# Two GpSimd drains among the last output scatters of a block-causal attention and mixture-of-experts kernel

## The chip, the cores and the metric

The kernel runs on one core of one Trainium2 chip, as one program with one launch. The metric is the device time of an execution in microseconds (us). Before the change the median of three executions is 787.66 us (785.13 to 788.49).

## The reference, cut to what matters

Attention of 8 batches and 8 heads with 576 positions of 64 elements comes first. Its mask is by blocks of 64 positions: a position sees its own block and all earlier ones. The 4608 rows of 512 elements that result are then sent to experts, each row to one expert, and each of the 8 experts takes 576 rows.

```python
attn = softmax(scale * q @ k.T, block-causal)          # 8 x 8 x 576 x 576
x = (attn @ v).transpose(0, 2, 1, 3).reshape(4608, 512)
logits = x @ w_gate                                    # 4608 x 8
for idx in np.argsort(-logits.flatten()):              # best pair (row, expert) first
    tok, e = idx // 8, idx % 8
    if assigned[tok] < 0 and counts[e] < 576: assigned[tok] = e; counts[e] += 1
for e in range(8):
    mask = assigned == e
    out[mask] = np.maximum(x[mask] @ w1[e], 0) @ w2[e] # 512 -> 1024 -> 512
```

## The kernel before, in words

The program has two stages. In the first, heads are worked off in pairs: TensorE makes the scores, VectorE and ScalarE the softmax, GpSimd a part of the scaling, and the result goes to a DRAM tensor `x` in 16-bit halves (a high part and a rest). In the second, a routing step finds for expert number `k` (0 to 7, in the order in which the routing fills them) the list of its 576 rows, the tile `ix`. Then the expert itself runs, and the next expert's routing runs beside it.

For each expert GpSimd (POOL) has three kinds of work. `gather` (L1006) fetches the expert's rows from `x` by five indirect DMAs, four of 128 rows and one of 64. `weights` (L977) makes the low halves of the weights, eight subtractions of 128x1024. `yev`, inside `ffn`, puts the results out: for each of five row tiles `m` TensorE finishes `y` (L1082, and L1086 for the tile of 64 rows), ScalarE scales it into the tile `yo` (L1065), for `m==4` VectorE adds a second half to it (L1069), and GpSimd issues one indirect DMA that scatters the rows of `yo` to the output in DRAM (L1073). That makes 40 gathers and 40 scatters in the program. The last expert takes its row tiles in the order 0, 1, 2, 4, 3, the others in the order 0 to 4; the fifth scatter of expert 6 is thus its tile of 64 rows, and so is the fourth scatter of expert 7.

All instructions are placed when the program is built. A greedy planner (class `Sched`) holds a model of the engines; every step is a generator that yields an engine, a cost and the events that it needs, and the planner decides which step comes next on which engine. What an engine then does at run time is its own list in that order, with semaphore waits between engines. What a step issues between two yields is placed together, and an instruction without a yield of its own has no cost in the planner's model.

Behind the last instruction the program has a closing part, put there by the context manager and shown in the profile under the line of the `_run` call (L1146): each engine drains, SyncE waits for the DMAs that are still out, all engines meet at a barrier, GpSimd clears the semaphores, and they meet again. The same kind of opening stands at the start under L1137.

Of the kernel before, what the change touches and what calls it, by code (L numbers as in the profile page):

```python
# [614 lines left out]
class Moe:  # L615
# [419 lines left out]
    def ffn(s,k):  # L1035
        nc=s.nc; fp=s.fp; sc=s.sc
        yield S,0,('xm',k,0),('xm',k,1 if k else 0),*[('wc',k,n) for n in range(4) if k or n==0]
        (W,Y),X=s.W[k],s.X[k]
        HH=fp.tile([P,8,576],F16,tag="HH",name=f"HH{k}",bufs=1); HL=fp.tile([P,8,576],F16,tag="HL",name=f"HL{k}",bufs=1)
        def hev(f,h,ps,gk,ts):  # L1040
            w=ts.stop-ts.start
            yield A,51+.835*w
            nc.scalar.activation(HH[:,f,ts],ps,AF.Relu)  # L1043
            yield D,69+1.042*w
            nc.vector.scalar_tensor_tensor(HL[:,f,ts],ps,0.0,HH[:,f,ts],op0=OP.max,op1=OP.subtract)  # L1045
            sc.set(('h',k,8*h+f)); sc.set(gk)
        for h,ts in enumerate((slice(0,256),slice(256,576)) if k else (slice(0,128),slice(128,576))):
            w=ts.stop-ts.start
            for f0 in range(0,8,4):
                pg={}  # L1050
                nf=4 if k==0 and h==0 and f0==0 else 1
                for f,d in [(f,d) for a in range(f0,f0+4,nf) for d in range(4) for f in range(a,a+nf)]:
                    yield T,3*(w/2.4+3),'g' if d==0 else None,('g2',k-1),*[('xm',k,m) for m in range(1,5) if h],('wc',k,d) if k==0 else None
                    if d==0: gk=sc.gtake(); pg[f]=s.ps.tile([P,512],F32,tag="g",name=f"h{k}_{f}_{h}",bufs=4)[:,:w],gk
                    ps,gk=pg[f]
                    for n,(a,l) in enumerate(((0,0),(0,2),(1,0))):
                        nc.tensor.matmul(ps,lhsT=W[:,a,d,f*P:f*P+P],rhs=X[:,4*(d//2)+d%2+l,ts],start=(d==0 and n==0),stop=(d==3 and n==2))  # L1057
                    sc.nolat()
                    if d==3: sc.add(hev(f,h,ps,gk,ts),1,sc.now+200)
        sca=1.0/(s.XS*s.WS*s.WS)  # L1060
        def yev(m,ps,gk):
            n=P if m<4 else 64
            yield A,478
            y=fp.tile([P,512],F32,tag="y",name=f"yo{k}_{m}",bufs=3)
            nc.scalar.activation(y[:n],ps[P-n:],AF.Copy,scale=sca)  # L1065
            if m==4:

                yield D,603
                nc.vector.scalar_tensor_tensor(y[:n],ps[:n],sca,y[:n],op0=OP.mult,op1=OP.add)  # L1069
            sc.set(gk)  # L1070

            yield G,1038,('yo',s.ny-1),('gi',1) if k==0 and m>1 else None
            nc.gpsimd.indirect_dma_start(out=s.out,out_offset=bass.IndirectOffsetOnAxis(ap=s.ix[k][:n,m:m+1],axis=0),in_=y[:n],in_offset=None)  # L1073

            sc.soft(728,('yo',s.ny)); sc.ev['yo',s.ny]=max(sc.ev['yo',s.ny],sc.now+4500); s.ny+=1
        for m in range(5) if k+1<s.E else (0,1,2,4,3):
            if m==0: sc.set(('mid',k))
            for f in range(8 if m<4 else 4):
                yield T,645 if m<4 else 720,*[(x,k,y) for g in ((f,) if m<4 else (f,f+4)) for x,y in (('h',g),('h',8+g),('wc',4+g//2))],'g' if f==0 else None
                if f==0: gk=sc.gtake(); ps=s.ps.tile([P,512],F32,tag="g",name=f"y{k}_{m}",bufs=4)  # L1080
                for n,(Z,a) in enumerate(((HH,0),(HH,1),(HL,0))):
                    if m<4: nc.tensor.matmul(ps,lhsT=Z[:,f,m*P:m*P+P],rhs=Y[:,a,f],start=(f==n==0),stop=(f==7 and n==2))  # L1082
                    else:

                        for g in range(2):
                            nc.tensor.matmul(ps[64*g:64*g+64],lhsT=Z[:,4*g+f,512:576],rhs=Y[:,a,4*g+f],start=(f==n==0),stop=(f==3 and n==2))  # L1086
                sc.nolat()
            if m==4: sc.set(('g2',k)); sc.set(('ffn',k))
            sc.add(yev(m,ps,gk),1,sc.now+200)
        if k+1<s.E: sc.add(s.ffn(k+1),3,sc.now)  # L1090
# [59 lines left out]
```

## Time and profile before

| what | value |
|---|---|
| three executions | 787.66 us median, 785.13 to 788.49 |
| the profiled execution's own time | 789.05 us |
| its span in the trace | 787.3 us |
| granted TensorE clock, mean over the span | 0.968 |

The span is the time from the first to the last record of the trace; 1.75 us of the profiled execution's own time lie outside it. Start times count from the span's start. POOL, ACT, DVE, PE and SP are GpSimd, ScalarE, VectorE, TensorE and SyncE; a name with a q behind it (POOLq, SPq) is the engine's own sequencer, whose rows (drains, semaphore waits) are not counted as busy time. The row of an indirect DMA on POOL is the time that GpSimd takes to issue it; the transfer itself is seen in the view of the DMA queues.

### The profile page before, as it was taken

The page shows a single profiled execution, that of the slowest core. Times are in us where ns is not written, and L with a number is a line of the kernel's source. Part 1 is how long each engine was busy: PE and PEld are TensorE (multiplying, and loading weights), DVE is VectorE, ACT ScalarE, POOL GpSimd, SP SyncE. Part 2 cuts the span into 40 slices and gives each one's busy share as a digit, 9 for nine tenths or more (in the row PEclk, how much of TensorE's full clock was granted, in tenths as well). Part 3 has the DMA queues.
Part 4 walks back from the last instruction along what each step waited for, and adds up shares of the span by engine and source line. Part 5 has one row for each costly group of instructions (what it writes and reads, how often), then busy time and mean ns, then how long its engine had stood idle before and what let it go on. Part 6 is the DMA issues. An engine that isn't in the chain of part 4 may idle for free.

```text
span 787.3 us, 19016 instructions
## 1 busy us (share of the span) xinstructions
PE 719.1 (91%) x6528; PEld 479.5 (61%) x6528; DVE 564.6 (72%) x2310; ACT 539.7 (69%) x1455; POOL 466.8 (59%) x509
## 2 busy tenths in 40 slices
PE   5879998999999999936999999999999999999995
PEld 3656776667776677734545747647557475574752
DVE  6899888998899879566988978869577693420210
ACT  5688888888998898724836868594965848392210
POOL 5788877898889777413414447283751926675001
PEclk9799999999999999975999999999999999999998
DMA  9878999989998993246117076472935719772001
GB/s 202 162 151 167 217 190 223 165 158 223 202 204 177 221 185 77 78 120 206 69 52 278 8 245 150 176 194 67 272 84 191 171 62 263 259 161 61 21 22 39
DMA packets 244305, 121.51 MB, mean 154 GB/s; under 512 B 200816, under 2 KB 227312, under 8 KB 244208
## 3 DMA queue, kind: packets, MB, share of 16 engines
q1 hardware_dynamic: 238320, 101.42, 57.1%
q0 software_dynamic: 5888, 18.88, 7.6%
q8 instruction: 51, 0.84, 0.4%
q14 instruction: 46, 0.38, 0.2%
HBM read 71.32 MB, written 18.87 MB: 115 GB/s over the span
## 4 chain that ended last, share of the span: by engine, by line
PE 38%; issue 5%; DMA 4%; ACT 4%; POOL 2%; DVE 0%; POOLq 0%; SPq 0%; ACTq 0%; DVEq 0%
PE h L1057 20%; PE y L1082 15%; DMA raw<-in_moe_w_dram 2%; PE y L1086 2%; POOL xg L1006 2%; ACT ja L752 1%; DMA out_dram<-yo,ix 1%; ACT W L975 1%; DMA xg<-x,ix 1%; ACT raw L971 1%; POOL W L977 1%; PE pe L934 1%; PE tot L824 0%; ACT yo L1065 0%; ACT HH L1043 0%
## 5 line engine op out<-in xcount | busy, mean ns | idle before, releaser
L438 POOL TENSOR_TENSOR P<-P,m 128x320 f32<-128x320 f32 (+8 forms) x285 | 209.5, 769 | 49.8 <-DVE m L430 32.6
L1057 PE MATMUL h<-X,W 128*128 128x320 f16 (+3 forms) x1536 | 196.0, 287 | 0.0
L416 ACT ACTIVATE P<-psb,m 128x576 f32<-128x576 f32 (+8 forms) x288 | 149.4, 542 | 26.7 <-DVE m L409 17.4
L1057 PEld LDWEIGHTS <-W 128*128 128x128 f16 x1536 | 141.9, 98 | 42.0 <-issue 2.7
L1082 PE MATMUL y<-W,HH 128*128 128x512 f16 x512 | 152.3, 379 | 0.0
L405 DVE TENSOR_REDUCE m<-psb 128x1 f32<-128x576 f32 (+8 forms) x288 | 125.0, 481 | 12.9 <-PE psb L380 12.4
L977 POOL TENSOR_TENSOR W<-raw,W 128x1024 f16<-128x1024 f32 x56 | 118.2, 2135 | 24.4 <-ACT W L975 21.4
L463 PE MATMUL psb<-mident,P 128*128 128x128 f32 x800 | 107.6, 283 | 11.3 <-POOL P L438 4.2
L1073 POOL DMA_INDIRECT out_dram<-yo,ix x40 | 39.3, 982 | 114.1 <-ACT yo L1065 82.0
L380 PEld LDWEIGHTS <-qT 128*64 128x64 f16 x1408 | 77.9, 113 | 42.9 <-issue 28.4
L463 PEld LDWEIGHTS psb<-mident,P 128*128 128x128 f32 x800 | 88.6, 144 | 22.9 <-POOL P L438 7.0
L380 PE MATMUL psb<-kT,qT 128*64 128x288 f16 (+8 forms) x704 | 91.7, 286 | 10.9 <-ACT P L416 9.8
L498 PE MATMUL psb<-PT,V 128*64 128x448 f32 (+5 forms) x776 | 98.1, 391 | 1.9 <-DVE PT L446 1.5
L1006 POOL DMA_INDIRECT xg<-x,ix x40 | 41.8, 1044 | 96.4 <-DMA raw<-in_moe_w_dram 49.8
L1043 ACT ACTIVATE HH<-h 128x320 f16<-128x320 f32 (+3 forms) x128 | 52.1, 410 | 65.8 <-PE h L1057 57.7
L1082 PE MATMUL y<-W,HL 128*128 128x512 f16 x256 | 97.0, 379 | 0.0
L444 ACT ACTIVATE PT<-psb 128x512 f32<-128x512 f32 (+1 forms) x165 | 82.4, 592 | 5.6 <-PE psb L463 5.4
L1045 DVE SCALAR_TENSOR_TENSOR HL<-h,HH 128x320 f16<-128x320 f32 (+3 forms) x128 | 57.3, 452 | 40.1 <-ACT HH L1043 36.3
L380 PE MATMUL psb<-kS,qT 128*64 128x288 f16 (+8 forms) x704 | 83.8, 283 | 0.3 <-DVE kS L350 0.2
L1082 PEld LDWEIGHTS <-HH 128*128 128x128 f16 x512 | 46.9, 98 | 53.9 <-issue 2.8
L971 ACT ACTIVATE raw<-raw 128x512 f32<-128x512 f32 x112 | 67.0, 624 | 6.9 <-DMA raw<-in_moe_w_dram 6.9
L498 PEld LDWEIGHTS psb<-PT,V 128*64 128x64 f32 x776 | 49.6, 138 | 33.2 <-issue 24.4
(216 smaller groups left out, 1037.3 us busy)
## 6 DMA issues: line engine op xcount, KB each, us to landing
raw<-in_moe_w_dram SPq DMA_DIRECT2D x64, 512.0 KB
x<-XR SPq DMA_DIRECT2D x8, 1152.0 KB
kn<-in_k_dram SPq DMA_DIRECT2D x15, 576.0 KB
qn<-in_q_dram SPq DMA_DIRECT2D x15, 576.0 KB
V<-in_v_dram SPq DMA_DIRECT2D x64, 128.0 KB
V<-in_v_dram SPq DMA_DIRECT2D x16, 64.0 KB
xg<-x,ix POOLq DMA_INDIRECT x40
out_dram<-yo,ix POOLq DMA_INDIRECT x40
```

Source lines behind the costliest of these rows:

```text
L380: nc.tensor.matmul(out if len(K1.shape) == 2 else out.rearrange("p (r j) -> p r j", r=2), lhsT=A[:, h, 64 * i:64 * i + 64], rhs=K1, start= ...
L405: nc.vector.tensor_reduce(m[:, 0, c:c + 1], ps[:, o:o + 64 * (i + 1)] if g else s.part(ps, g, i, o), axis=AX.X if g else AX.XY, op=OP.max)
L416: nc.scalar.activation(out, in_, AF.Exp, bias=m[:, 1, c:c + 1], scale=s.ESC, accum_out=m[:, 2, c:c + 1])
L438: nc.gpsimd.tensor_tensor(sl, sl, m[:, 3, c:c + 1].to_broadcast([P, w]), op=OP.mult)
L444: s.nc.scalar.activation(out, in_, AF.Copy)
L463: nc.tensor.transpose(ps[:, a], s.Pb[n % s.NP][:, s.OFF[i] + 128 * j:s.OFF[i] + 128 * j + P], s.ident)
L498: nc.tensor.matmul(ps[64 * h:64 * h + 64, 64 * (i0 - b0):64 * (b1 - b0)], lhsT=vn[:, j, 2 * (n % 2) + h, :], rhs=pt[:, s.PTI[(j, i0)]:s.PT ...
L971: nc.scalar.activation(raw[:,x],raw[:,x],AF.Copy,scale=s.WS)
L977: nc.gpsimd.tensor_tensor(lw,raw,hi,op=OP.subtract)
L1006: nc.gpsimd.indirect_dma_start(out=xg[:n],out_offset=None,in_=s.xd,in_offset=bass.IndirectOffsetOnAxis(ap=ix[:n,m:m+1],axis=0))
L1057: nc.tensor.matmul(ps,lhsT=W[:,a,d,f*P:f*P+P],rhs=X[:,4*(d//2)+d%2+l,ts],start=(d==0 and n==0),stop=(d==3 and n==2))
L1082: if m<4: nc.tensor.matmul(ps,lhsT=Z[:,f,m*P:m*P+P],rhs=Y[:,a,f],start=(f==n==0),stop=(f==7 and n==2))
```

## The change

One line is added to `yev`. Behind the scatter of row tile 4, for the experts 6 and 7, GpSimd gets a drain instruction. It is issued without a yield, so that the planner does not know of it, and the order of all other instructions is the same as before on every engine. Lines below it have numbers that are higher by one (the closing part is at L1147).

```diff
@@ yev, behind the scatter (L1073)
             yield G,1038,('yo',s.ny-1),('gi',1) if k==0 and m>1 else None
             nc.gpsimd.indirect_dma_start(out=s.out,out_offset=bass.IndirectOffsetOnAxis(ap=s.ix[k][:n,m:m+1],axis=0),in_=y[:n],in_offset=None)
 
+            if m==4 and k>s.E-3: nc.gpsimd.drain()
             sc.soft(728,('yo',s.ny)); sc.ev['yo',s.ny]=max(sc.ev['yo',s.ny],sc.now+4500); s.ny+=1
```

The list of GpSimd from the end of expert 6 on is now: scatter of tile 4 of expert 6, drain, scatters of tiles 0, 1, 2 and 4 of expert 7, drain, scatter of tile 3 of expert 7, and then the drain of the closing part.

## The prediction

> **What bounds the kernel now.** I read the page's busy shares first, then the end of the chain of waits, then GpSimd's rows in order of time, then the rows of the closing part, because the change touches nothing but GpSimd's list in the last 60 us.
>
> From the page: TensorE carries the program.
>
> ```profile
> span 787.3 us, 19016 instructions
> PE 719.1 (91%) x6528; PEld 479.5 (61%) x6528; DVE 564.6 (72%) x2310; ACT 539.7 (69%) x1455; POOL 466.8 (59%) x509
> ```
>
> TensorE is busy for 91% of the span, so GpSimd, with 59%, matters only where TensorE has ended. That is the end. The last pieces of the chain of waits (start, length, what):
>
> ```profile
> 773.35 0.69 DVE yo L1069
> 774.33 2.60 DMA out_dram<-yo,ix
> 776.97 1.67 issue
> 778.64 1.20 POOLq L1146
> ```
>
> The chain runs through the last scatters into a piece of GpSimd's own sequencer in the closing part. It shows 1.20 us of that piece and stops at 779.84, while the span goes on to 787.3. What fills the rest is in the rows of line L1146, the closing part (count, then shortest/median/longest in ns, then first and last start in us):
>
> ```profile
> L1146 SPq EVENT_SEMAPHORE  x13: 17/28/28, 773.6 to 787.2; - x13
> L1146 POOLq EVENT_SEMAPHORE  x4: 17/17/17, 786.5 to 787.2; - x4
> L1146 POOLq DRAIN  x3: 45/108/7803, 778.6 to 787.0; - x3
> L1146 ACTq DRAIN  x2: 14/310/607, 778.0 to 786.7; - x2
> ```
>
> One of GpSimd's three closing drains takes 7.803 us. It is the first of them, since the chain starts its piece at 778.64, so it ends at 786.44. GpSimd's first barrier step follows at 786.5, and the span ends 0.8 us later. The drain is therefore the last thing that the barrier waits for. ScalarE's longest is 0.607 us and ends at 778.6 with its last copy. Now GpSimd's own rows in order of time (start, length, idle time before it in brackets):
>
> ```profile
> 729.00 0.96 POOL L1073 DMA_INDIRECT out_dram<-yo,ix  x1 [4.27 <-ACT yo L1065]
> 732.47 0.90 POOL L1073 DMA_INDIRECT out_dram<-yo,ix  x1 [2.51 <-DVE yo L1069]
> 760.52 0.96 POOL L1073 DMA_INDIRECT out_dram<-yo,ix  x1 [27.14 <-ACT yo L1065]
> 765.70 0.96 POOL L1073 DMA_INDIRECT out_dram<-yo,ix  x1 [4.22 <-ACT yo L1065]
> 770.83 0.96 POOL L1073 DMA_INDIRECT out_dram<-yo,ix  x1 [4.17 <-ACT yo L1065]
> 774.33 0.91 POOL L1073 DMA_INDIRECT out_dram<-yo,ix  x1 [2.54 <-DVE yo L1069]
> 778.88 0.96 POOL L1073 DMA_INDIRECT out_dram<-yo,ix  x1 [3.64 <-ACT yo L1065]
> ```
>
> The last scatter's row ends at 778.88 + 0.96 = 779.84. From there to the end of the drain at 786.44 are 6.60 us in which GpSimd has no row but the drain. Is it the transfer that the drain waits for? The DMA view of 779.9 to 782.3, in 40 slices of 0.06 us, and SyncE's rows in two windows (778.5 to 782.0, then 782 to 783) say no:
>
> ```profile
> DMA  0000000099598599799500000000000000000000
> DMA packets 80, 0.26 MB, mean 109 GB/s; under 512 B 16, under 2 KB 16, under 8 KB 80
> L1146 SPq EVENT_SEMAPHORE  x7: 28/28/28, 781.6 to 782.0; - x7
> L1146 SPq DRAIN  x2: 7/10/13, 782.2 to 782.2; - x2
> ```
>
> The last packet is through at 779.9 + 20 x 0.06 = 781.1. SyncE, which waits for the completion of each outstanding DMA in turn, gets the last one at 781.6 and stands at the barrier at 782.2. All that the output needs is done then; GpSimd's drain holds the program until 786.44, which is 4.2 us longer.
>
> **The change part by part.** The edit adds two drains to GpSimd's list and takes nothing away. What they do hangs on where the 6.60 us come from, and the trace of before has no drain among scatters. The nearest rows are the two ends of the bound. At the low end stands the opening drain under L1137, behind four memsets and ahead of any DMA:
>
> ```profile
> L1137 POOLq DRAIN  x1: 169/169/169, 0.3 to 0.3; - x1
> L1006 POOL DMA_INDIRECT xg<-x,ix x40 | 41.8, 1044 | 96.4 <-DMA raw<-in_moe_w_dram 49.8 <-DVE ix L944 19.1 <-ACT W L964 15.9
> L1073 POOL DMA_INDIRECT out_dram<-yo,ix x40 | 39.3, 982 | 114.1 <-ACT yo L1065 82.0 <-ACT HH L1043 6.9 <-DVE jk L810 6.8
> ```
>
> A drain with no indirect DMA ahead of it takes 0.169 us, and the two that follow the long one in the closing part, with no DMA between, take 0.108 and 0.045 us. The long one stands behind 40 gathers and 40 scatters with no drain in 787 us. So there are two readings, with a price f for the part of the 6.60 us that a drain pays each time behind a scatter. In the first, f is near nothing and the 6.60 us are a debt that grows with the indirect DMAs since the last drain: 6.60 / 80 = 0.083 us for each. In the second, f is the whole 6.60 us, whatever lies ahead. I take the first: rows of 0.9 to 1.0 us for issues that move only 128 rows leave it natural that some bookkeeping for each stays behind, and a fixed wait that goes on 4.8 us after the transfer's completion (781.6 to 786.44) has nothing in the trace to wait for. That is a choice between readings, not a measurement.
>
> Under the first reading:
> - The first added drain follows the scatter at 732.47, whose row ends at 733.37. It pays for 75 DMAs, 75 x 0.083 = 6.2 us, and ends at 739.6. Queued behind it on GpSimd is only the scatter at 760.52, which waits for ScalarE anyway. The cover is the gap of 27.14 us, in which TensorE works without GpSimd. Cost 0; without that cover it would be 6.2 us.
> - The second follows the scatter at 774.33, whose row ends at 775.24. It pays for 4 DMAs, 0.33 us, and ends at 775.6. Behind it waits only the last scatter, which starts at 778.88 when ScalarE's `yo` is there. The cover is 778.88 - 775.24 = 3.64 us. Cost 0.
> - The closing drain pays for one DMA: it ends at 779.84 + 0.08 = 779.9 in place of 786.44.
>
> What is late next is SyncE, at the barrier at 782.2. It does not move, since the last scatter doesn't. The view of the stretches (window, its length, then busy time of PE, PEld, DVE, ACT, POOL) shows the first cover and the empty end: in the gap behind expert 6 TensorE is busy throughout and GpSimd idle, and behind the last scatter no engine has work left:
>
> ```profile
> 733.40:760.50 27.10, 27.10 (x199) 19.23 (x198) 6.91 (x15) 6.78 (x16) 0.00 (x0) 1.00 0.03 6
> 779.84:787.30 7.46, 0.00 (x0) 0.00 (x0) 0.00 (x0) 0.00 (x0) 0.00 (x0) 0.61 0.09 35
> ```
>
> Behind the drain the closing part still takes 787.3 - 786.44 = 0.82 us (two barriers and the clearing of semaphores between them), and I add 0.05 us for the way of SyncE's signal. New end of the span: 782.23 + 0.05 + 0.82 = 783.1. The gain is 787.3 - 783.1 = 4.2 us, not 6.60, because SyncE's wait for the last scatter takes over. In the profiled execution that makes 789.05 - 4.2 = 784.85. The median of the runs is 1.39 us under that execution; the tail is the same instructions there, so I take the 4.2 us off the median: **783.5 us**.
>
> For a general f the sum has three pieces. Up to f = 2.4 (782.2 less 779.84) the closing drain still hides behind SyncE and the gain is the full 4.2. From 2.4 to 3.64 the gain is 6.60 - f. Above 3.64 the second added drain pushes the last scatter by f - 3.64 and the closing drain costs f again, so the time changes by (f - 3.64) + (f - 6.60) = 2f - 10.24: nothing is gained at f = 5.12, and at f = 6.60 it is a loss of 2.96 us.
>
> **The rivals.**
>
> First, the slower one: f is fixed. Each drain behind a scatter takes 6.60 us, so the second added one ends at 775.24 + 6.60 = 781.84 and the last scatter, ready at 778.88, starts there. Everything behind it moves by 2.96 us: 787.66 + 2.96 = 790.6. For it speaks that the only long drain in the trace is also the only one directly behind a scatter, so the trace cannot part debt from fixed price; against it, that nothing recorded lasts as long. It decides from f above 5.12. The Trainium skill, page "GPSIMD Engine Reference", section on instruction dispatch, says that the first call of freshly loaded code costs about 6 us with no instruction shown; if such a load came with each drain among scatters, an estimate from that page's figure of 5.95 us would be 2 x 5.95 - 10.24 = 1.7 us of loss. No run here shows such a load, and the opening drain of 0.169 us shows none at its place. Chance 0.17.
>
> Second, a mixture: f lies between 2.4 and 5.1, say a fixed wait of 3 to 5 us and a debt on top. The gain is then between 4.2 and nothing, 783.5 to 787.7, about 784.5 in the middle of it (f = 3.4, gain 3.2). For it speaks that a drain may well wait for the scatter's completion (781.6, that is 1.8 us behind its row) and then have work of its own; f would be 1.8 us and some more. Chance 0.13.
>
> Third, the change does not do what it must do: the added drains return at once and leave the debt to the closing one. The time stays at 787.7. This is what would happen if a drain ended as soon as the engine's last row has ended and the 6.60 us belonged to the program's end. The Trainium skill, page "PSUM — Partial Sum Buffer", section "Engine vs sequencer instructions", says that a drain waits until the engine is fully idle; by that rule, with idle read as the end of the last row, the closing drain would end at 779.84. The trace disagrees with that reading: it ends at 786.44, so something without a row counts as work. Against this rival speaks that the closing drain is a drain like the others. Chance 0.10.
>
> **How the numbers follow.** The forecast has 0.60, the fixed price 0.17, the mixture 0.13, no effect 0.10. The three runs lie 2.5 us under to 0.8 us over their median, so I give the forecast its own range of 781.8 to 785.2. It, the mixture and no effect together hold 0.83; the range that reaches to no effect, with some of that scatter, is 781.8 to 788.9, and the fixed price is left out.
>
> The bound of 0.5% (about what a measurement of this kernel can tell from no change) is 3.94 us, so faster by it means under 783.72. The forecast lies only 0.2 us beyond that: of its 0.60 I put 0.36 there, and 0.02 from the mixture: 0.38. Slower by it means over 791.6, which the fixed price with its 2.96 us reaches only by scatter: 0.05. The rest, 0.57, is within the bound.
>
> **What would show it right or wrong.** In the profile after, line L1075 has two drains on POOLq. If the first is around 7 us long (the scatter's own 0.9 us, then 6.2) and the second and the closing one are each under about 1.5 us, with the scatter's issue included, the debt is shown. The last scatter must still start 3.6 us behind the end of the scatter before it, and the span must end about 0.9 us behind SyncE's drain. Two long added drains and a last scatter that starts more than 6 us behind the end of the one before would show the fixed price. Short added drains beside a closing drain of 7.8 us would show that they do nothing. My number is wrong in size alone if the closing drain still ends behind SyncE's.

## The result, and the profile after

The changed kernel takes 781.14 us (median of 7 executions, 779.81 to 783.17); the kernel before takes 785.13 us on the same chip (median of 7, 784.58 to 788.49). The ratio is 0.9945, with a 95% interval of 0.9929 to 0.996: faster by 0.55%, or about 4.3 us, where 4.2 us were forecast. The predicted time of 783.5 us was too high all the same, and the measured one lies 0.66 us under the range, because the level of before from which the 4.2 us were taken was 787.66 us, the median of the first three executions. 785.13 - 4.2 would have been 780.9. The ratios here and below are of undisturbed executions alone; the profiled executions of the first two experiments were slow ones (795.58 and 797.95 us), so of those two only the tail and the drains are read.

The profiled execution of the changed kernel has a span of 778.0 us, 9.3 us less than before, and most readers will stop at that number. It is not the effect. From the page:

```profile
span 778.0 us, 19018 instructions
PE 713.4 (92%) x6528; PEld 476.5 (61%) x6528; DVE 565.1 (73%) x2310; ACT 539.2 (69%) x1455; POOL 465.4 (60%) x509
```

The same 6528 matmuls took 5.7 us less TensorE time in this execution, at a granted clock of 0.980 against 0.968. To take that out I compare only the tail: the stretch from the end of the last matmul to the end of the span. The last matmul rows of before and of after:

```profile
777.54 0.38 PE L1082 MATMUL y<-W,HL 128*128 128x512 f16 x1
```

```profile
772.53 0.38 PE L1083 MATMUL y<-W,HL 128*128 128x512 f16 x1
```

Before, the tail runs from 777.92 to 787.26, 9.34 us; after, from 772.91 to 778.03, 5.12 us. That is 4.22 us less, which agrees with the ratio. Now the drains after: the added ones (line L1075), GpSimd's issues around them, and the closing part (L1147), the last two rows from a window of 777.0 to 777.3.

```profile
L1075 POOLq DRAIN  x2: 3021/5174/7327, 727.2 to 769.1; - x2
```

```profile
727.46 0.90 POOL L1073 DMA_INDIRECT out_dram<-yo,ix  x1 [2.51 <-DVE yo L1069]
755.51 0.96 POOL L1073 DMA_INDIRECT out_dram<-yo,ix  x1 [27.15 <-ACT yo L1065]
...
769.33 0.90 POOL L1073 DMA_INDIRECT out_dram<-yo,ix  x1 [2.55 <-DVE yo L1069]
773.87 0.96 POOL L1073 DMA_INDIRECT out_dram<-yo,ix  x1 [3.63 <-ACT yo L1065]
```

```profile
L1147 POOLq DRAIN  x3: 51/108/3026, 773.6 to 777.8; - x3
L1147 SPq DRAIN  x2: 7/10/13, 777.2 to 777.2; - x2
L1147 POOLq EVENT_SEMAPHORE  x1: 17/17/17, 777.3 to 777.3; - x1
```

A drain's row begins shortly before the scatter that it waits for, so its length says little; what counts is how far its end lies behind the end of the scatter's row. (The view prints a drain's start to a tenth of a microsecond; the ends given here are the trace's own, to its nanoseconds.) The first added drain ends at 734.57, which is 6.20 us behind the scatter's 728.36. The second ends at 772.13, 1.90 us behind 770.23, and the scatter after it starts with the idle time that it had before (3.63 against 3.64 us). The closing drain is down from 7.80 to 3.03 us and ends at 776.66, 1.83 us behind the scatter's row in place of 6.61 (6.60 by the rounded times of the prediction). SyncE's drain at 777.2 is now later than GpSimd's, and the barrier follows at once.

### The profile page after: what moved, and what is told of

It reads as the page before. It is cut to its first block, busy times and chain, and to the rows that moved or that the text cites. A ratio compares the mean times of both kernels' runs of the same rounds, so it can differ in the third digit from the quotient of the medians.

```text
span 778.0 us, 19018 instructions
## 1 busy us (share of the span) xinstructions
PE 713.4 (92%) x6528; PEld 476.5 (61%) x6528; DVE 565.1 (73%) x2310; ACT 539.2 (69%) x1455; POOL 465.4 (60%) x509
## 3 DMA queue, kind: packets, MB, share of 16 engines
q0 software_dynamic: 5888, 18.88, 7.5%
## 4 chain that ended last, share of the span: by engine, by line
PE 42%; DMA 5%; POOL 2%; ACT 2%; issue 2%; DVE 1%; SPq 0%; POOLq 0%; ACTq 0%; DVEq 0%
PE h L1057 22%; PE y L1083 17%; DMA raw<-in_moe_w_dram 3%; PE y L1087 2%; POOL xg L1006 1%; DMA xg<-x,ix 1%; POOL W L977 1%; PE pe L934 1%; ACT ja L752 1%; ACT W L975 0%; ACT raw L971 0%; PE tot L824 0%; DMA out_dram<-yo,ix 0%; ACT yo L1065 0%; ACT HH L1043 0%
## 5 line engine op out<-in xcount | busy, mean ns | idle before, releaser
L380 PE MATMUL psb<-kT,qT 128*64 128x288 f16 (+8 forms) x704 | 89.7, 281 | 11.6 <-ACT P L416 10.8
L380 PE MATMUL psb<-kS,qT 128*64 128x288 f16 (+8 forms) x704 | 82.0, 278 | 1.6 <-DVE kS L350 1.5
```

The source lines that it names most:

```text
L380: nc.tensor.matmul(out if len(K1.shape) == 2 else out.rearrange("p (r j) -> p r j", r=2), lhsT=A[:, h, 64 * i:64 * i + 64], rhs=K1, start= ...
```

## The experiments

The theory: a drain on GpSimd waits for the last indirect DMA to complete and pays, besides, a debt that grows with the number of indirect DMAs since the last drain. The rivals: a cost of the first drain among scatters, whatever lies ahead of it (the first was long, the later ones short); a debt of time or of other GpSimd instructions; a debt of rows or packets; and the second added drain as the one that does the work. In the tables below n is the number of indirect DMAs since the last drain. Executions of one kernel differ from chip to chip and run to run by more than the effect, so single executions are read by their tails alone.

**The first drain alone.**

```diff
-            if m==4 and k>s.E-3: nc.gpsimd.drain()
+            if m==4 and k==s.E-2: nc.gpsimd.drain()
```

> Only the drain behind the fifth scatter of expert 6 is kept. Debt theory (a drain waits for the completion of the last indirect DMA, some 1.8 us behind the scatter's row, and pays about 0.06 us for each further indirect DMA since the last drain): the closing drain has 5 DMAs to pay for and ends about 2.1 us behind the last scatter's row, ahead of SyncE's last wait (2.4 us), so the time is that of the changed kernel, 4.2 us under before. First-call theory (the first drain among scatters is long whatever lies ahead, later ones are short): the same time, closing drain 1.8 us behind the row. Rival that the second added drain is what shortens the closing one: closing drain 6.6 us behind the row and the time of before.

Measured: 786.30 us (median of all 7) against 791.13 us (median of 18) for before on this chip, ratio 0.9938 (0.9909 to 0.9968). Its last scatter and its closing drain:

```profile
789.61 0.96 POOL L1073 DMA_INDIRECT out_dram<-yo,ix  x1 [3.64 <-ACT yo L1065]
```

```profile
L1147 POOLq DRAIN  x3: 51/108/3193, 789.4 to 793.5; - x3
L1147 SPq DRAIN  x3: 7/7/13, 792.9 to 793.2; - x3
```

The closing drain pays for 5 DMAs and ends at 789.376 + 3.193 = 792.57, 2.00 us behind the scatter's row (2.1 expected) and ahead of SyncE at 792.9. The tail is 5.12 us, as with both drains. The second added drain does nothing for the time.

**The second drain alone.**

```diff
-            if m==4 and k>s.E-3: nc.gpsimd.drain()
+            if m==4 and k==s.E-1: nc.gpsimd.drain()
```

> Only the drain behind the fourth scatter of expert 7 is kept. Debt theory: it pays for 79 indirect DMAs, ends about 6.5 us behind the scatter's row where 3.64 us are covered, so the last scatter starts about 2.9 us later (6.6 us behind the end of the one before it, not 3.64); the closing drain is short (1.8 us behind the row) and the time is 4.2 - 2.9 = 1.3 us under before. First-call theory: the same. If the time were that of the changed kernel, the position of the long drain would not matter.

Measured: 793.25 us (median of all 12), ratio 1.0004 (0.9979 to 1.0028), no difference. The forecast of 1.3 us (0.9984) lies in that interval, so the ratio decides nothing; the rows do:

```profile
783.78 0.90 POOL L1073 DMA_INDIRECT out_dram<-yo,ix  x1 [2.56 <-DVE yo L1069]
792.00 0.96 POOL L1073 DMA_INDIRECT out_dram<-yo,ix  x1 [7.32 <-issue]
```

```profile
L1075 POOLq DRAIN  x1: 7653/7653/7653, 783.6 to 783.6; - x1
```

The drain has 79 DMAs to pay for, ends 6.53 us behind the scatter's row, as forecast, and the last scatter starts 7.32 us behind that row in place of 3.64. It is 3.7 us late and not 2.9, because from the end of the drain (791.21) to the start of the scatter there are another 0.8 us. In them GpSimd's sequencer goes through the semaphore wait of the scatter, which ends at 791.27, and the scatter starts 0.73 us behind that. This is not a price of the drain. In the trace of before, without any drain, 11 of the 36 scatters that have such a wait start 0.72 to 0.73 us behind its end, and none starts sooner. One of them, whose tile had been written by 680.4:

```profile
L1073 POOLq EVENT_SEMAPHORE  x1: 4856/4856/4856, 680.3 to 680.3; - x1
685.86 0.96 POOL L1073 DMA_INDIRECT out_dram<-yo,ix  x1 [3.97 <-ACT HH L1043]
```

That wait ends at 685.14, 0.73 us ahead of the scatter. The cover of 3.64 us was therefore too long by 0.79 us: in this gap a drain is free up to 2.85 us behind the scatter's row. The tail is 8.81 us: 0.53 us shorter than before in place of 1.3. Of the 4.22 us of gain 3.7 are paid back where the cover is missing.

**A drain for every expert.**

```diff
-            if m==4 and k>s.E-3: nc.gpsimd.drain()
+            if m==4: nc.gpsimd.drain()
```

> A drain behind the scatter of row tile 4 of all eight experts. Indirect DMAs since the last drain: 15 at the first, 10 at the next six but the last, then 4, and 1 at the closing one. Debt after the completion: the first drain ends about 2.7 us behind the scatter's row, those with 10 about 2.4 us. Debt side by side with the completion (0.08 us for each, from the row's end): all end at the completion, 1.8 to 1.9 us. First-call theory: the first ends 6 us or more behind the row, all others 1.8 to 1.9 us. In all three the time is close to that of the changed kernel.

Measured, one execution: 786.51 us, tail 5.12 us. The first of its drains and the scatter ahead of it, then all eight:

```profile
434.04 0.91 POOL L1073 DMA_INDIRECT out_dram<-yo,ix  x1 [4.06 <-DVE jk L810]
```

```profile
L1075 POOLq DRAIN  x1: 3486/3486/3486, 433.8 to 433.8; - x1
...
L1075 POOLq DRAIN  x8: 3019/3273/5177, 433.8 to 775.8; - x8
```

The first drain has 15 DMAs and ends 2.35 us behind its scatter's row, not 6: the first-call theory has fallen. The six with 10 DMAs end 2.13 to 2.14 us behind. That lies between the two forms of debt that I had in mind (2.4 and 1.8 to 1.9). Two of these six have rows of 5.1 and 5.2 us and are no exception: they were reached while two weight subtractions were still running.

**A drain ahead of any indirect DMA, and one that leaves 25.**

```diff
+            if k==0 and m==0: nc.gpsimd.drain()          # ahead of the first gather
...
-            if m==4 and k>s.E-3: nc.gpsimd.drain()
+            if m==4 and k==s.E-4: nc.gpsimd.drain()
```

> One drain ahead of the first gather (no indirect DMA before it, but more than 300 other GpSimd instructions and half of the span), and one behind the fifth scatter of expert 4; the two of the change are left out. Debt after the completion: the first takes about 0.1 us beyond the work ahead of it; the second pays for 55 and ends about 5.1 us behind the scatter's row; the closing one pays for 25 and ends 3.3 us behind the last scatter's row, 0.9 us behind SyncE, so the time is about 3.3 us under before. Debt side by side with the completion: 0.1 us, 4.6 us, 2.2 us, and 4.2 us under before. First-call theory: the drain ahead of the gathers takes 6 us and all later ones end 1.8 to 1.9 us behind the row. A debt of time or of other GpSimd instructions: the drain ahead of the gathers takes some us.

Measured, one execution: 789.17 us, tail 5.56 us. The drain ahead of the gathers with the two GpSimd rows before it, then the one behind expert 4 with its scatter, then the closing one with its:

```profile
341.71 1.01 POOL L709 TENSOR_SCALAR m_Lm<-logits,sc_g 128x288 f32<-128x288 f32 x1 [2.16 <-DVE sc_g L705]
342.80 1.25 POOL L710 TENSOR_SCALAR PV<-m_Lr,sc_g 128x288 f32<-128x288 f32 x1
...
641.06 0.91 POOL L1074 DMA_INDIRECT out_dram<-yo,ix  x1 [2.54 <-DVE jk L810]
...
782.75 0.96 POOL L1074 DMA_INDIRECT out_dram<-yo,ix  x1 [3.64 <-ACT yo L1066]
```

```profile
L1004 POOLq DRAIN  x1: 2461/2461/2461, 341.7 to 341.7; - x1
L1076 POOLq DRAIN  x1: 5692/5692/5692, 640.8 to 640.8; - x1
L1148 POOLq DRAIN  x3: 51/108/4017, 782.5 to 787.1; - x3
L1148 SPq DRAIN  x3: 7/7/13, 786.0 to 786.8; - x3
```

The first ends at 344.12, 0.07 us behind the work ahead of it, after 342 us and 324 subtractions and multiplications of two tiles on GpSimd: time and other instructions leave no debt. The second (55 DMAs) ends 4.57 us behind its scatter's row, where the two forms had given 5.1 and 4.6. The closing one (25) ends at 786.54, which is 2.82 us behind its row, between the 3.3 and 2.2 expected, and 0.42 us behind SyncE's drain at 786.11. The tail is 5.56 us, 0.44 longer than with the change, which is that lag: where the closing drain is later than SyncE, it shows in the time one for one. The trace of before says the same, with a lag of 4.22 us and a tail that is 4.22 us longer.

**More indirect DMAs, hardly more rows.**

```diff
             if m==4: sc.set(('gi',k))
+            for j in range(5 if m==4 and 0<k<7 else 0):
+                xs=fp.tile([16,1024],F16,tag="xs",name=f"xs{k}_{j}",bufs=5)
+                nc.gpsimd.indirect_dma_start(out=xs[:16],out_offset=None,in_=s.xd,in_offset=bass.IndirectOffsetOnAxis(ap=ix[:16,j:j+1],axis=0))
```

> The kernel before with 30 more indirect DMAs and no added drain: behind the gathers of experts 1 to 6, five more of 16 rows each, into a scratch tile that nothing reads. The closing drain then follows 110 indirect DMAs, whose rows are 9696 in place of 9216. Debt for each indirect DMA (0.08 us where many are owed): closing drain about 9.0 us behind the last scatter's row, in place of 6.6. Debt for each row moved: 6.9 us. Debt for each packet (720 more on 5888): 7.4 us.

Measured, one execution: 828.63 us; the added gathers cost some 40 us elsewhere in the program, which I did not follow up. Its last scatter and its closing drain:

```profile
816.02 0.96 POOL L1076 DMA_INDIRECT out_dram<-yo,ix  x1 [3.67 <-ACT yo L1068]
```

```profile
L1149 POOLq DRAIN  x3: 51/108/10248, 815.8 to 826.6; - x3
```

It ends at 826.04, 9.05 us behind the scatter's row, with 9.0 expected for a debt of each DMA. The packets on the indirect queue rose to 6848 (960 more, not the 720 of my expectation), which would give 6.6 x 6848 / 5888 = 7.7 us. It is the number of DMAs that counts, not rows or packets. A gather and a scatter weigh the same: the 30 added gathers cost 2.44 us, 0.081 each, and the five scatters from 75 to 80 owed 0.41 us, 0.081 each.

**The change once more.** The kernel is the changed one, unedited.

> The changed kernel once more, to see whether its gain is the same on another day's level of the runs: from the two traces' tails 4.2 us, a ratio of 0.9947, whatever the median of before is here. If the level of the runs were part of the effect, the ratio would move with it.

Measured: 782.98 us (median of 12) against 788.37 us (median of 17) for before on that chip, ratio 0.9946 (0.9928 to 0.9964). The tail is 5.12 us again. The level moved by over 3 us, the ratio did not.

The drains behind a scatter, one for each n (those that repeat an n agree with it within 0.01 us), by the end of the drain less the end of the scatter's row:

| n | us behind the row | run |
|---|---|---|
| 1 | 1.83 | changed kernel |
| 4 | 1.90 | changed kernel |
| 5 | 2.00 | first drain alone |
| 10 | 2.13 | every expert |
| 15 | 2.35 | every expert |
| 25 | 2.82 | 25 left |
| 55 | 4.57 | 25 left |
| 75 | 6.20 | changed kernel |
| 79 | 6.53 | second drain alone |
| 80 | 6.61 | before |
| 110 | 9.05 | small gathers |

From 55 on a straight line through the rows is 0.12 + 0.081 n, within 0.02 us; up to 25 it is 1.79 + 0.041 n, within 0.07 us. By these two lines the price of a DMA where few are owed is half of that where many are. Idle time does not work the debt off: the drains with 79 and 80 owed came after GpSimd's idle gap of 27 us, the one with 75 ahead of it, and all three lie on the same line.

## Why the prediction was right in its mechanism and wrong in its number

- **The closing drain holds the end.** Right. It went from 7.80 to 3.03 us, and the tail lost 4.22 us.
- **A debt for each indirect DMA, 0.083 us.** That there is such a debt is right, and shown by the table: 0 DMAs leave 0.07 us, 110 leave 9.05. For 75 the forecast of 6.2 us met 6.20, but that tests little, since the price came from the drain with 80. In proportion to n it holds only where many are owed: 15 would give 1.25 us, and 2.35 were measured.
- **"f is near nothing".** Wrong in size. A drain behind one scatter still ends 1.83 us behind its row, where I had put 0.08 us, and behind four 1.90, where I had 0.33. By the prediction's own sign the debt was shown if the second and the closing drain were each under 1.5 us long; they were 3.02 and 3.03 us, so it took the later runs to show it. The ends are close to the time at which the scatter's completion reaches SyncE (781.6 in the trace of before, 1.8 us behind that scatter's row). It cost nothing, because 1.83 is under the 2.4 us at which SyncE stands at the barrier. The sum had named that limit; that f, put near nothing, stayed 0.57 us inside it was luck.
- **What is late next is SyncE.** Right: 777.2 against GpSimd's 776.66. From there to the span's end 0.80 us passed, 0.87 were allowed.
- **Both covers hold.** Right: 27.15 us against 6.20, 3.63 against 1.90, also with the 0.79 us taken off each cover that a scatter needs behind a drain and that the sum left out. But the second drain was not needed for the gain, which the sum did not say.
- **The rivals.** The fixed price (2.96 us slower) and no effect fell in the first trace, and so did the mixture, which put f between 2.4 and 5.1. Its ground, that a drain may wait for the scatter's completion 1.8 us behind the row, is near the measured f of 1.83 us. The ground of the fixed price, that one long drain cannot part debt from price, was sound, and f has in fact a fixed part; it is 1.8 us and not above 5.12. The Trainium skill's page "GPSIMD Engine Reference", section on instruction dispatch, gives about 6 us for a first call of freshly loaded code. No drain here shows one: the first drain among scatters with 15 DMAs owed ended 2.35 us behind its scatter's row, and the one ahead of any indirect DMA 0.07 us behind the work before it.
- **The step that failed** is the level in "I take the 4.2 us off the median", and the range laid around it. The term 787.66 us was the median of three executions; with four more of the same kernel the median was 785.13 us, and 4.2 us off that is 780.9. The low end of the range was put at 781.8, 1.7 us under the forecast, although the prediction had itself noted that the three executions reach 2.5 us under their median: 783.5 - 2.5 = 781.0 would have held the measured 781.14. Before had medians of 785.13, 791.13 and 788.37 us in the three sets with more executions, so an absolute time carries a level of some 3 us to either side that three executions did not show. On which side it fell was chance. The difference was right: 4.22 us in the tail, where 4.2 were forecast.

## What to carry to other kernels

Look behind the last busy row: a drain in the closing part can be the last thing on the chip, and an equal drain placed earlier, in a gap where its engine is idle and ahead of the last few indirect DMAs, takes that work out of the tail. Such a drain must be covered in full, with the 0.8 us that the next scatter needs behind it, since in a short gap it pushes the work queued behind it. One is enough if what is left for the closing one stays under the next wait. When an effect is half a per cent, compare stretches of the two traces that the change can touch, and state the absolute level with the spread of levels, not of three executions.

## What the runs showed of the hardware that was not expected

- By the two fits the price of an indirect DMA in a drain has two values, 0.041 us each with up to 25 owed and 0.081 us with 55 and more. One form that gives both: half of the work runs while the last scatter is still under way, and is hidden by it when little is owed; the other half follows. That is a fit to eleven rows; the cause is not shown.
- None of the 36 scatters of before that have a semaphore wait of their own starts sooner than 0.72 us behind its end, with the tile ready or not. That time is hidden where the tile comes late, and it shows behind a drain that is not covered, where it came to 0.79 us from the drain's end (791.21) to the scatter's start (792.00).
